# Linear attention and a feed-forward layer on one core: k^T v by heads in column halves, matmuls in the gaps of the head, additions on GpSimd, other urgencies for the planner

## The chip, the cores and the metric

The kernel runs on one core of one Trainium2 chip. The metric is the device time of that core in microseconds, the median of several executions. The engines are TensorE (PE in the profile, its weight loads apart as PEld), VectorE (DVE), ScalarE (ACT), GpSimd (POOL) and SyncE (SP), which issues most transfers.

## The reference

Eight batches of eight heads, 576 positions, head dimension 64. `q`, `k` and `v` are float32, the two weight matrices come in as float64.

```python
q_s = softmax(q, axis=-1)              # over the head dimension
k_s = softmax(k, axis=2)               # over the positions
kv = np.einsum('bhsd,bhse->bhde', k_s, v)          # 64 x 64 for each head
attn = np.einsum('bhsd,bhde->bhse', q_s, kv)
x = attn.transpose(0, 2, 1, 3).reshape(4608, 512)
h = np.maximum(x @ w_in, 0.0)          # w_in 512 x 2048
out = h * h @ w_out                    # w_out 2048 x 512
```

## The kernel before

The output is made in nine tiles `t` of 512 rows: the first 512 positions of each of the eight batches, and a last tile of the eight tails of 64 positions. A tile runs over 16 slices `f` of 128 columns of the hidden layer. For one slice, `first` makes `h` with 12 matmuls, `split_g` squares it and splits it into a high and a low part `gh`, `gl`, and `second` adds 12 matmuls into the four accumulators `acc` of the tile. Each factor is a sum of two float32r parts, and three products of parts are added: that is where the 12 come from. While tile `t` runs, the attention of batch `t + 1` is prepared between its slices (`step`, `step_after`), one pair of heads `p` in four slices.

`kv_product` makes k^T v for such a pair: it multiplies the exponentials of `k` (128 positions by 2 x 64 columns, in `ek`) with `v` of both heads, over four chunks of 128 positions and one more for the tail. The 128 x 128 result holds the two heads' products on its diagonal, and the other two blocks are not used. From batch 1 on, `v` carries a column of ones between its heads (129 columns), so that the sums of the softmax come out of the same matmul. These factors are plain float32; the profile shows each such matmul as two passes.

The weights come as 64-bit words (`load_words`) and are turned into two float32r parts in 16 units: `scale_words` on ACT, `join_words` (a shift and a bit merge on DVE, then an addition of 32-bit integers), `split_words` (a cast on ACT, a subtraction on POOL). In half of the units (even ones), the addition of the first half runs on DVE (`on_vector`), all others on POOL.

Everything up to the end of the loop over slices of tile 0 is recorded and not issued: batch 0's attention ("the head" below), the words, tile 0 and batch 1's attention. `Planner.run` gives every recorded piece a start time from its costs, taking of the pieces that could start next on an engine the one with the longest way to the end (`tail`), and then issues all pieces in the order of these starts. All later code is issued in the order in which it stands. So each engine works through one fixed list, and a piece late in it waits for all before.

The head, for each of four pairs: `first_max` turns `k` with four PE transposes (`kT`), `first_exp` takes exponentials (ACT), `first_turn` turns them back (`ek`, and `ekt` for the tail), `q_norm` and `q_turn` do the same for `q` (`qT`), `kv_product`, and `x_product` (six matmuls of 288 columns) gives a quarter of tile 0's `x`. Line 99 of the profile is the helper that issues every recorded or direct call.

Of the kernel before, what the change touches and what calls it, by code (L numbers as in the profile page):

```python
# [2 lines left out]

# [6 lines left out]
F32 = mybir.dt.float32  # L10
# [103 lines left out]
class Node:  # L114


    def __init__(self, engine):
        self.engine, self.calls, self.busy, self.moved = engine, [], 0.0, 0
        self.before, self.after, self.soon = {}, {}, []
        self.buffers, self.behind = [], None  # L120
        self.start = self.end = self.tail = None


class Planner:
# [3 lines left out]

    HOP = 0.12
    ISSUE, LAND, RATE = 0.6, 2.0, 330.0  # L130
    WAIT = 0.25

    def __init__(self):
        self.open, self.nodes, self.into, self.chain, self.boot = True, [], None, None, []
        self.marks, self.line = {}, {}
        self.due, self.dues = None, []

    @contextmanager
    def together(self, chained=False):
# [16 lines left out]
    def add(self, engine, call, busy, moved, views):  # L156
        if self.into in (None, "next"):
            node = Node(engine)
            self.nodes.append(node)
            if self.into:  # L160
                self.into = node
        else:
            node = self.into
        if moved and self.line is not None:
            node.behind = self.line.get(engine)
            self.line[engine] = node
        if self.due is not None:
            self.dues.append((node, self.due))
        node.calls.append(call)
        node.busy += busy  # L170
        node.moved += moved
        for view, written in views:
            b = view.buffer
            if not b.users and not b.choices:
                told = b.pool.told.setdefault(b.tag, [])
                depth = b.bufs or b.pool.depth
                b.last = told[-1] if told else None
                b.before = told[-depth] if len(told) >= depth else None
                told.append(b)
            if node not in b.users:  # L180
                b.users.append(node)
                node.buffers.append(b)
                if b.pool is not None and b.pool.early:
                    self.boot.append(node)
            for other, w, touched in b.seen:
                if other is not node and (w or written) and (
                    touched is None or view.touched is None or touched & view.touched
                ):
                    node.before[other] = True
            b.seen.append((node, written, view.touched))  # L190
# [43 lines left out]
            ) and all(self.possible(o, b, known, spare) for o in n.before)  # L234
        return known[n]

    def run(self):
        for n in self.nodes:
            for o in n.before:
                o.after[n] = True  # L240
        for n, f in self.dues:
            n.soon = [self.marks[f]] if f in self.marks else []
        for n in self.nodes:
            self.length(n)
        for n in self.nodes:
            for b in n.buffers:
                if len(b.choices) > 1 and n is not b.users[0]:
                    n.tail = max(n.tail, *[u.tail for u in b.users[1:]])
        left = {n: len(n.before) for n in self.nodes}
        ready = [n for n in self.nodes if not left[n]]  # L250
        free, dma, told = {}, 0.0, []
        self.banks = {}
        while ready:
            able = []
            for n in ready:
                t = free.get(n.engine, 0.0)
                if n.behind is not None:
                    if n.behind.start is None:
                        continue
                    t = max(t, n.behind.start + n.behind.busy)  # L260
                for o in n.before:
                    t = max(t, o.end + (0.0 if o.engine is n.engine and not o.moved else self.HOP))
                for b in n.buffers:
                    if b.placed is not None:
                        continue
                    at, _ = self.place(b)
                    if at is None:
                        break
                    t = max(t, at + self.HOP)
                else:  # L270
                    able.append((t, n))
            t0, n0 = min(able, key=lambda x: x[0])
            t, n = max(
                ((t, n) for t, n in able if n.engine is n0.engine and t <= t0 + self.WAIT),
                key=lambda x: x[1].tail,
            )
            n.start, n.end = t, t + n.busy
            free[n.engine] = n.end
            if n.moved:
                dma = max(dma, n.end) + n.moved / self.RATE  # L280
                n.end = dma + self.LAND
            for b in n.buffers:
                if b.placed is None:
                    b.placed = t
                    if b.choices:
                        b.pool, b.tag = self.place(b)[1]
                        self.banks[b.tag] = float("inf")
            for b in n.buffers:
                if b.choices and all(u.end is not None for u in b.users):
                    self.banks[b.tag] = max(u.end for u in b.users)  # L290
            told.append(n)
            ready.remove(n)
            for o in n.after:
                left[o] -= 1
                if not left[o]:
                    ready.append(o)
        assert len(told) == len(self.nodes)
        self.open = False
        for n in sorted(told, key=lambda n: n.start):
            for call in n.calls:  # L300
                call()

# [2 lines left out]
def attention_ffn(  # L305
# [25 lines left out]
    nc = tc.nc  # L331
# [14 lines left out]
    LA = 2  # L346
    LINE = 5
    SOON = 4
    EARLY = 2
    SH = SQ // 2  # L350
    TB = 2
# [85 lines left out]
    def join_words(f):  # L437
        w = cvt.tile([P, 2, M], I32, tag="w", name=f"w_{f}")
        for h in range(2):
            at = slice(h * M, (h + 1) * M)  # L440
            lo, hi = part(f, I32, 0, [h])[:, at], part(f, I32, 1, [h])[:, at]
            ps = bank(f"up_{f}_{h}", f < EARLY).bitcast(I32)
            to = w[:, h, :].only(h)
            V.tensor_scalar(
                out=ps, in0=hi, scalar1=3, scalar2=None, op0=ALU.logical_shift_left
            )
            on_vector = h == 0 and f % 2 == 0
            V.scalar_tensor_tensor(
                out=ps if on_vector else to, in0=hi, scalar=-(2**31), in1=ps,
                op0=ALU.bitwise_and, op1=ALU.bitwise_or,  # L450
            )
            (V if on_vector else G).tensor_tensor(
                out=to, in0=ps if on_vector else to, in1=lo, op=ALU.add, n=580
            )
# [384 lines left out]
    def kv_product(b, p):  # L839
# [2 lines left out]
        tl, th = tail_of(b, p)  # L842
        ps = bank(f"kv_{b}_{p}", b == 0)
        w = 2 * D if b == 0 else W
        with plan.together():
            for c in range(C):
                T.matmul(
                    out=ps[:, 0:w], lhsT=kr[:, c, :], rhs=vr[:, :, c, :] if b == 0 else vr[:, c, :],
                    start=(c == 0), stop=False, n=4 * w,
                )  # L850
            if b == 0:
                T.matmul(
                    out=ps[:, 0:w], lhsT=made.pop(("ekt", p)),
                    rhs=v_heads[tl, 2 * p:2 * p + 2, 0:D].only(p // 2),
                    start=False, stop=True, n=4 * w,
                )
            else:
                T.matmul(
                    out=ps[:, 0:w],
                    lhsT=made["kt", b][:, th, :].rearrange("p h d -> p (h d)").only(  # L860
                        p % 2, p % 2 + 2
                    ),
                    rhs=v_tail[:, p * (W + 1):p * (W + 1) + W],
                    start=False,
                    stop=True,
                    n=4 * w,
                )
        if b == 0:
            ks, at_of = made.pop(("ks", p)), D
        else:  # L870
# [161 lines left out]
        first_turn(p)  # L1032

    for p in range(NP):
        boot_max(p)
        boot_turn(p)
        boot_exp(p)
        q_norm(0, p, G)
        kv_product(0, p)
        q_turn(0, p)  # L1040
        x_product(0, p, x)
    done = {scale_words: 0, join_words: 0, split_words: 0}

    def convert(work, until):
        for u in range(done[work], min(until + 1, NF)):
            work(u)
            done[work] = u + 1

    for u in range(LINE, NF):
        load_words(u)  # L1050
# [72 lines left out]
                prepare(b, p + 1)  # L1123

    prepare(1, 0)
    x_next = None
    for t in range(B + 1):
        b = t + 1
# [27 lines left out]
                step_after(b, f, x_next)  # L1156
            plan.due = None
        if t == 0:
            plan.run()
        if b <= B:  # L1160
            x = split_x(x_next, b)
        if b + 1 < B:
# [43 lines left out]
```

## Time and profile before

| | |
|---|---|
| median of 3 runs | 895.93 us (894.77 to 896.78) |
| the profiled execution | 895.74 us, its span 893.8 us |
| granted TensorE clock, mean | 0.997 |
| PE busy / DVE / ACT / POOL | 871.8 / 483.6 / 358.6 / 187.1 us |

The span reaches from the first to the last instruction; 1.9 us of the profiled execution lie outside it. The busy share is the time in which an engine has an instruction open: matmuls are pipelined, so the durations of neighbouring ones overlap, and the distance between the starts of two rows says what a matmul costs. A granted clock of 1 is 2.4 GHz, one of 0.5 is 1.2 GHz.

### The profile page before, as it was taken

Reading aid. Unit: us, or ns where it says so; the run is one execution under the profiler, and the core shown is the slowest. Engines: PE = TensorE matmul, PEld = TensorE weight load, DVE = VectorE, ACT = ScalarE, POOL = GpSimd, SP = SyncE. Lnnn points to the kernel's source line nnn. Section 1 sums busy time; section 2 is a strip of 40 time slices with the busy share of each in tenths; the row PEclk is TensorE's granted clock in tenths of the full one; section 3 lists DMA queues with packets and bytes.
Section 4 is the critical chain, followed back from the end, with each engine's and each line's share of the span. In section 5 each row is a group of like instructions: output and inputs, shape, how many; then the busy total and the mean of one; then the engine's idle time right before and its main releaser. Section 6 shows DMA issues by size and latency. Waiting matters only on the chain.

```text
span 893.8 us, 11668 instructions
## 1 busy us (share of the span) xinstructions
PE 871.8 (98%) x4054; PEld 725.0 (81%) x4054; DVE 483.6 (54%) x907; ACT 358.6 (40%) x668; POOL 187.1 (21%) x223
## 2 busy tenths in 40 slices
PE   5899999999999999999999999999999999999997
PEld 3777888888888888888888888888888888888886
DVE  7899996544654456544655555446545522233222
ACT  5788854333433243333433343333433422232221
POOL 4477871111011111111111111110111100000000
PEclk9999999999999999999999999999999999999999
DMA  9991022111321123112321122113211020010002
GB/s 282 383 317 49 23 55 84 39 38 27 92 48 38 38 56 86 38 38 50 83 47 28 36 80 49 38 27 76 65 38 38 9 93 1 0 48 1 1 0 48
DMA packets 140874, 57.84 MB, mean 65 GB/s; under 512 B 115600, under 2 KB 134032, under 8 KB 140688
## 3 DMA queue, kind: packets, MB, share of 16 engines
q1 hardware_dynamic: 139104, 55.79, 23.3%
q10 hardware_dynamic: 1712, 1.31, 0.5%
q8 instruction: 32, 0.52, 0.2%
q14 instruction: 26, 0.21, 0.1%
HBM read 46.14 MB, written 10.49 MB: 63 GB/s over the span
## 4 chain that ended last, share of the span: by engine, by line
PE 91%; DVE 5%; issue 1%; ACT 1%; DMA 0%; ACTq 0%; POOL 0%; DVEq 0%; POOLq 0%
PE h L99 42%; PE acc L99 42%; PE kv L99 4%; PE x L99 3%; DVE up L99 1%; DVE w L99 1%; DVE km L99 1%; DMA q<-in_q_dram 0%; DVE h L99 0%; PE qT L99 0%; DVE gl L99 0%; DVE qt L99 0%; DVE mx L99 0%; ACT raw L99 0%; ACTq L99 0%
## 5 line engine op out<-in xcount | busy, mean ns | idle before, releaser
L99 PE MATMUL h<-xh,w 128*128 128x512 f32 x1152 | 380.3, 393 | 1.9 <-DVE gl L99 1.9
L99 PE MATMUL acc<-w,gh 128*128 128x512 f32 x1152 | 355.6, 390 | 0.0
L99 PEld LDWEIGHTS h<-xh,w 128*128 128x128 f32 x1152 | 216.6, 188 | 48.3 <-DVE gl L99 3.3
L99 PEld LDWEIGHTS acc<-w,gh 128*128 128x128 f32 x1152 | 215.1, 188 | 43.9
L99 PE MATMUL h<-xl,w 128*128 128x512 f32 x576 | 225.0, 391 | 0.3 <-DVE xl L99 0.3
L99 PE MATMUL acc<-w,gl 128*128 128x512 f32 x576 | 224.1, 389 | 0.0
L99 DVE SCALAR_TENSOR_TENSOR h<-h,r 128x512 f32<-128x512 f32 x144 | 99.6, 692 | 120.5 <-ACT r L99 120.1
L99 DVE TENSOR_TENSOR gl<-h,gh 128x512 fp32r<-128x512 f32 x144 | 99.2, 689 | 114.2 <-ACT gh L99 111.4
L99 ACT ACTIVATE r<-h 128x512 f32<-128x512 f32 x144 | 85.5, 593 | 171.0 <-PE h L99 170.8
L99 ACT ACTIVATE gh<-r 128x512 fp32r<-128x512 f32 x144 | 90.6, 629 | 124.2 <-PE acc L99 121.9
L99 PEld LDWEIGHTS acc<-w,gl 128*128 128x128 f32 x576 | 108.1, 188 | 22.7
L99 PEld LDWEIGHTS h<-xl,w 128*128 128x128 f32 x576 | 108.4, 188 | 21.5 <-DVE xl L99 0.6
L99 POOL TENSOR_TENSOR k<-k,kmx 128x512 f32<-128x512 f32 x24 | 30.8, 1283 | 170.5 <-issue 134.1
L99 POOL PARTITION_ALL_REDUCE kmx<-km x24 | 17.4, 725 | 197.7 <-DVE km L99 162.5
L99 ACT ACTIVATE q<-q 128x576 f32<-128x576 f32 (+1 forms) x32 | 21.5, 672 | 88.3 <-DVE q L99 82.9
L99 POOL TENSOR_TENSOR ql<-qT,qh 128x576 fp32r<-128x576 f32 x24 | 34.1, 1422 | 104.3 <-issue 54.7
L99 POOL TENSOR_TENSOR w<-w,w 128x512 fp32r<-128x512 f32 x32 | 41.0, 1300 | 16.7 <-ACT w L99 16.7
L99 PEld LDWEIGHTS kv<-v,ek 128*128 128x128 f32 x256 | 34.8, 199 | 3.5 <-DVE ql L99 1.3
L99 DVE SCALAR_TENSOR_TENSOR bsm<-bsm,sw_s 128x18 f32<-128x18 f32 x24 | 4.6, 191 | 60.9 <-DMA sw_s<-bsm 60.9
L99 ACT CAST qh<-qT 128x576 fp32r<-128x576 f32 (+1 forms) x32 | 20.7, 650 | 41.1 <-DVE qT L99 41.1
L99 PE MATMUL kv<-v,ek 128*128 128x129 f32 (+1 forms) x256 | 35.7, 284 | 1.1 <-DVE ql L99 1.1
L99 ACT ACTIVATE raw<-raw 128x1024 f32<-128x1024 f32 (+1 forms) x32 | 35.7, 1144 | 0.1
(103 smaller groups left out, 649.4 us busy)
## 6 DMA issues: line engine op xcount, KB each, us to landing
k<-in_k_dram SPq DMA_DIRECT2D x32, 256.0 KB, 2.7
raw<-in_moe_w_in_dram SPq DMA_DIRECT2D x16, 512.0 KB, 7.8
raw<-in_moe_w_out_dram SPq DMA_DIRECT2D x16, 512.0 KB, 9.2
out_dram<-o SPq DMA_DIRECT2D x32, 256.0 KB, 2.4
v<-in_v_dram SPq DMA_DIRECT2D x56, 128.0 KB, 2.9
q<-in_q_dram SPq DMA_DIRECT2D x96, 72.0 KB, 2.3
sw_m<-bmx SPq DMA_DIRECT2D x96, 2.2 KB, 1.7
sw_s<-bsm SPq DMA_DIRECT2D x96, 2.2 KB, 1.7
```

What stands on the lines that cost most here:

```text
L99: getattr(self.eng, op)(*map(real, args), **{k: real(a) for k, a in kwargs.items()})
```

## The change

`kv_product` makes each chunk with two matmuls instead of one: each takes the 64 columns of one head from `ek` and the 64 (or 65, with the ones) columns of that head from `v`, and writes rows 0 to 63 or 64 to 127 of the result. The two take their places in two column halves of TensorE's array. A product is then 10 matmuls of 64 stationary columns, in place of 5 of 128, and the unused blocks are not made. The planner's cost for them is halved in the same way.

`join_words` does all additions on GpSimd (`on_vector` is always false).

The planner gets three things. Its urgencies (`tail`) are shifted by random amounts on 32 random stretches of its list, given by fixed seeds. Where its plan has TensorE idle ahead of a piece, up to the first matmul of the first `h`, it issues transposes of the identity matrix into a PSUM tile that nothing reads (`fill`), as many as fit the planned gap at 0.25 us each in the first gap and 0.14 us each later. `STEP` and `EASE` are zero, so `ease` does nothing.

```diff
+    READY, COLD, FILL, SPARE = 1.0, 0.25, 0.14, 0.2
...
+    def shift(self, seed):
+        r = random.Random(seed)
+        at, size, by = r.randrange(len(self.nodes)), r.randint(1, 40), r.gauss(0.0, 5.0)
+        for n in self.nodes[at:at + size]:
+            n.tail += by
...
+        first, free = min(m.start for m in self.marks.values()), self.READY
         for n in sorted(told, key=lambda n: n.start):
+            if n.engine is self.marks[0].engine and n.start <= first:
+                fill(int((n.start - free - self.SPARE) / (self.FILL if free > self.READY else self.COLD)))
+                free = n.end
             for call in n.calls:
                 call()
...
+    SEEDS = (1,6,7,10,14,16,17,42,48,79,152,157,158,195,310,373,389,455,905,9005,9006,9011,9012,9022,9044,9049,9071,9080,9087,9120,9132,9219,9227)
...
-            on_vector = h == 0 and f % 2 == 0
+            on_vector = False
...
+            parts = [(kr[:, c, :], vr[:, c, :]) for c in range(C)] + [(ekt, v_tail[:, at:at + W])]
+
+        n = D if b == 0 else D + 1
         with plan.together():
-            for c in range(C):
-                T.matmul(
-                    out=ps[:, 0:w], lhsT=kr[:, c, :], rhs=vr[:, :, c, :] if b == 0 else vr[:, c, :],
-                    start=(c == 0), stop=False, n=4 * w,
-                )
+            for i, (k_part, v_part) in enumerate(parts):
+                for j in range(2):
+                    rows, cols = slice(j * D, (j + 1) * D), slice(j * D, j * D + n)
+                    T.matmul(
+                        out=ps[rows, cols], lhsT=k_part[:, rows],
+                        rhs=vr[:, j, i, :] if b == 0 else v_part[:, cols],
+                        start=(i == 0), stop=(b > 0 and i == C), n=2 * n,
+                    )
...
+    def fill(n):
+
+        for _ in range(n):
+            nc.tensor.transpose(out=idle[:, 0:P], in_=ident, identity=ident)
```

TensorE's list begins with batch 0's transposes; the digit behind `k_` and `qn_` is the pair of heads. Before:

```order
L99 MATMUL kT_131<-ident,k_0_110 128x128 x4
L99 MATMUL ktT<-ident,kt_114 128x128 x2
L99 MATMUL kT_153<-ident,k_1_120 128x128 x4
L99 MATMUL ek_177<-ident,k_0_110 128x128 x4
L99 MATMUL ekt_186<-ident,kt_114 128x128
L99 MATMUL ek_217<-ident,k_1_120 128x128 x4
L99 MATMUL qT_0_238<-ident,qn_0_223 128x128 x4
L99 MATMUL qT_1_249<-ident,qn_1_234 128x128 x4
L99 MATMUL ekt_268<-ident,kt_114 128x128
L99 MATMUL kv_0_285<-v_0_126,ek_0_188 128x128 x4
L99 MATMUL kv_0_285<-v_tail,ekt_279 128x128
```

And with the change, over the same stretch:

```order
L1173 MATMUL idle<-ident 128x128 x9
L100 MATMUL kT_141<-ident,k_0_111 128x128 x4
L1173 MATMUL idle<-ident 128x128 x4
L100 MATMUL ktT<-ident,kt_115 128x128 x2
L1173 MATMUL idle<-ident 128x128 x3
L100 MATMUL kT_170<-ident,k_1_121 128x128 x4
L1173 MATMUL idle<-ident 128x128 x27
L100 MATMUL ek_240<-ident,k_0_111 128x128 x4
L100 MATMUL ekt_250<-ident,kt_115 128x128
L1173 MATMUL idle<-ident 128x128 x11
L100 MATMUL ek_284<-ident,k_1_121 128x128 x4
L100 MATMUL qTt_294<-ident,qt_117 128x128 x2
```

There are 84 such fillings in all, 54 of them ahead of the second `ek`, 30 more in three places behind the first two products. Both products of the first two pairs now stand one behind the other.

In later batches the list keeps its order, and only the product changes. This is pair 2 of batch 2, before:

```order
L99 MATMUL acc_3_1712<-w_1094,gh_8_2033 128x512 x2
L99 MATMUL acc_3_1712<-w_1094,gl_8_2035 128x512
L99 MATMUL kv_2_2120<-v_2_1934,ek_2_2072 128x129 x4
L99 MATMUL kv_2_2120<-v_tail,kt_1489 128x129
L99 MATMUL h_11_2137<-xh_0_1551,w_1094 128x512
```

and with the change:

```order
L100 MATMUL acc_3_1837<-w_1176,gh_8_2168 128x512 x2
L100 MATMUL acc_3_1837<-w_1176,gl_8_2170 128x512
L100 MATMUL kv_2_2255<-v_2_2069,ek_2_2207 64x65 x8
L100 MATMUL kv_2_2255<-v_tail,kt_1627 64x65 x2
L100 MATMUL h_11_2277<-xh_0_1676,w_1250 128x512
```

Five matmuls with 128 stationary columns have become ten with 64; what stands ahead and behind is the same.

On VectorE the first unit of words stood between the sums of `q` in the head (`up` is the shifted word, `w` the merged one, `ISA` the addition on DVE):

```order
L99 TENSOR_REDUCE sm_2_236<-q_2_124 128x8
L99 TENSOR_SCALAR up_1_247<-raw_137 128x512
L99 TENSOR_SCALAR up_0_256<-raw_137 128x512
L99 SCALAR_TENSOR_TENSOR w_262<-raw_137,up_1_247 128x512
L99 SCALAR_TENSOR_TENSOR up_0_256<-raw_137,up_0_256 128x512
L99 ISA w_262<-raw_137,up_0_256 128x1024
L99 COPY ekt_279<-ekt_186 64x128
L99 TENSOR_REDUCE sm_3_283<-q_3_128 128x8
```

and it now stands behind them:

```order
L100 COPY ekt_297<-ekt_250 64x128
L100 COPY ekt_303<-ekt_299 64x128
L100 SCALAR_TENSOR_TENSOR ks_0_205<-ks_0_205 128x1
L100 RECIPROCAL ks_0_205<-ks_0_205 128x1
L100 TENSOR_REDUCE sm_2_317<-q_2_125 128x8
L100 TENSOR_REDUCE sm_3_331<-q_3_129 128x8
L100 TENSOR_SCALAR sm_3_331<-sm_3_331 128x8
L100 RECIPROCAL sm_3_331<-sm_3_331 128x8
L100 TENSOR_SCALAR up_0_356<-raw_147 128x512
L100 SCALAR_TENSOR_TENSOR w_362<-raw_147,up_0_356 128x512
L100 TENSOR_SCALAR up_1_367<-raw_147 128x512
L100 SCALAR_TENSOR_TENSOR w_362<-raw_147,up_1_367 128x512
```

What the first two products need (`ekt`, `ks`) has moved ahead of the words, and the addition has left this engine.

## Rows read from the trace of the kernel before

**Rows 1.** The page's line of busy time: us, share of span, instructions.
```profile
PE 871.8 (98%) x4054; PEld 725.0 (81%) x4054; DVE 483.6 (54%) x907; ACT 358.6 (40%) x668; POOL 187.1 (21%) x223
```

**Rows 2.** Stretches: us, then busy by engine (instructions), clock, DMA share, GB/s.
```profile
10.00:42.00 32.00, 25.40 (x121) 20.27 (x121) 29.01 (x72) 24.71 (x56) 16.47 (x23) 0.95 1.07 368
42.00:138.00 96.00, 92.65 (x441) 75.75 (x442) 88.78 (x158) 71.77 (x108) 73.75 (x70) 1.00 0.39 116
138.00:410.00 272.00, 272.00 (x1281) 228.05 (x1280) 146.59 (x279) 100.37 (x199) 43.82 (x56) 1.00 0.21 49
```

**Rows 3.** TensorE's timeline around one product of batch 3: start, us, instructions.
```profile
321.14 0.39 PE L99 MATMUL acc<-w,gl 128*128 128x512 f32 x1
321.37 1.05 PE L99 MATMUL kv<-v,ek 128*128 128x129 f32 x8
322.26 0.39 PE L99 MATMUL kv<-v_tail,kt 128*128 128x129 f32 x2
322.40 0.48 PE L99 MATMUL h<-xh,w 128*128 128x512 f32 x1
322.71 0.40 PE L99 MATMUL h<-xl,w 128*128 128x512 f32 x1
```

**Rows 4.** Groups by line and form: busy us, mean ns of one, idle before.
```profile
L99 PE MATMUL kv<-v,ek 128*128 128x129 f32 x224 | 29.6, 274 | 0.0
```

**Rows 5.** TensorE's timeline in the head, idle time ahead in brackets.
```profile
9.99 1.11 PE L99 MATMUL ek<-ident,k 128*128 128x128 f32 x4
...
14.40 1.11 PE L99 MATMUL ek<-ident,k 128*128 128x128 f32 x4 [3.08 <-ACT k L99]
15.69 2.13 PE L99 MATMUL qT<-ident,qn 128*128 128x128 f32 x8 [0.18 <-POOL qn L99]
18.09 0.47 PE L99 MATMUL ekt<-ident,kt 128*128 128x128 f32 x1 [0.27 <-ACT ek L99]
18.36 2.00 PE L99 MATMUL kv<-v,ek 128*128 128x128 f32 x8
20.29 0.79 PE L99 MATMUL kv<-v_tail,ekt 64*128 64x128 f32 x2
21.01 0.69 PE L99 MATMUL qTt<-ident,qt 128*128 128x128 f32 x2
21.49 1.91 PE L99 MATMUL kv<-v,ek 128*128 128x128 f32 x8
...
24.06 1.05 PE L99 MATMUL kT<-ident,k 128*128 128x128 f32 x4
24.82 0.42 PE L99 MATMUL x<-qh,kvh 128*128 128x288 f32 x1
25.08 0.30 PE L99 MATMUL x<-ql,kvh 128*128 128x288 f32 x1
25.21 0.29 PE L99 MATMUL x<-qh,kvl 128*128 128x288 f32 x1
...
29.93 1.16 PE L99 MATMUL kv<-v,ek 128*128 128x128 f32 x8 [1.09 <-DVE ql L99]
31.02 0.48 PE L99 MATMUL kv<-v_tail,ekt 64*128 64x128 f32 x2
31.43 0.86 PE L99 MATMUL kT<-ident,k 128*128 128x128 f32 x4
```

**Rows 6.** Stretches of 2 us (columns as in group 2).
```profile
30.00:32.00 2.00, 2.00 (x15) 1.76 (x15) 1.89 (x7) 1.39 (x3) 0.00 (x0) 0.94 1.05 395
32.00:34.00 2.00, 2.00 (x11) 1.98 (x10) 1.95 (x5) 0.70 (x3) 1.43 (x2) 0.50 1.06 406
34.00:36.00 2.00, 2.00 (x12) 1.75 (x11) 1.34 (x3) 1.45 (x5) 0.28 (x2) 0.71 1.09 404
```

**Rows 7.** Groups by line and form: the additions of the words.
```profile
L99 POOL TENSOR_TENSOR w<-w,raw 128x512 int32<-128x512 int32 x24 | 31.3, 1312 | 8.4 <-DVE w L99 4.1 <-ACT ek L99 1.7 <-ACT qh L99 1.5
L99 DVE CUSTOM_DVE_ANT_0 w<-raw,up 128x1024 uint16<-128x1024 uint16 x8 | 5.4, 681 | 0.3
```

More of the change, by code (lines that the diff above doesn't have):

```diff
@@ L1 @@
 import itertools
+import random
 from contextlib import ExitStack, contextmanager
@@ L121, in __init__ @@
         self.start = self.end = self.tail = None
+        self.since = 0.0
 class Planner:
@@ L136, in __init__ @@
         self.due, self.dues = None, []
+        self.ease = 0.0
     @contextmanager
@@ L166, in add @@
             self.line[engine] = node
+        node.ease = self.ease
         if self.due is not None:
@@ L235, in possible, with prepare @@
         return known[n]
-    def run(self):
+    def prepare(self):
         for n in self.nodes:
@@ L248, in run, with order @@
                     n.tail = max(n.tail, *[u.tail for u in b.users[1:]])
+        for n in self.nodes:
+            n.tail -= n.ease
+    def order(self):
         left = {n: len(n.before) for n in self.nodes}
+        for n in self.nodes:
+            n.since, n.start, n.end = 0.0, None, None
+            for b in n.buffers:
+                b.placed = None
         ready = [n for n in self.nodes if not left[n]]
@@ L255, in run @@
             for n in ready:
-                t = free.get(n.engine, 0.0)
+                t = max(free.get(n.engine, 0.0), n.since)
                 if n.behind is not None:
@@ L260, in run @@
                     t = max(t, n.behind.start + n.behind.busy)
-                for o in n.before:
-                    t = max(t, o.end + (0.0 if o.engine is n.engine and not o.moved else self.HOP))
                 for b in n.buffers:
@@ L294, in run @@
                 left[o] -= 1
+                o.since = max(
+                    o.since, n.end + (0.0 if o.engine is n.engine and not n.moved else self.HOP)
+                )
                 if not left[o]:
                     ready.append(o)
+        return told
+    def shift(self, seed):
[3 more added lines that the diff above has]
+            n.tail += by
+    def run(self, seeds, fill):
+        self.prepare()
+        for seed in seeds:
+            self.shift(seed)
+        told = self.order()
         assert len(told) == len(self.nodes)
         self.open = False
+        first, free = min(m.start for m in self.marks.values()), self.READY
         for n in sorted(told, key=lambda n: n.start):
+            if n.engine is self.marks[0].engine and n.start <= first:
+                fill(int((n.start - free - self.SPARE) / (self.FILL if free > self.READY else self.COLD)))
+                free = n.end
             for call in n.calls:
@@ L348, in attention_ffn @@
     SOON = 4
+    STEP = 0.0
+    SEEDS = (1,6,7,10,14,16,17,42,48,79,152,157,158,195,310,373,389,455,905,9005,9006,9011,9012,9022,9044,9049,9071,9080,9087,9120,9132,9219,9227)
+    EASE = 0.0
     EARLY = 2
@@ L844, in kv_product @@
         w = 2 * D if b == 0 else W
-        with plan.together():
-            for c in range(C):
-                T.matmul(
-                    out=ps[:, 0:w], lhsT=kr[:, c, :], rhs=vr[:, :, c, :] if b == 0 else vr[:, c, :],
-                    start=(c == 0), stop=False, n=4 * w,
-                )
-            if b == 0:
[L852 to L867, printed above, removed]
+        if b == 0:
+            ekt = made.pop(("ekt", p))
+            parts = [(kr[:, c, :], None) for c in range(C)]
+        else:
+            ekt = made["kt", b][:, th, :].rearrange("p h d -> p (h d)").only(p % 2, p % 2 + 2)
+            at = p * (W + 1)
+            parts = [(kr[:, c, :], vr[:, c, :]) for c in range(C)] + [(ekt, v_tail[:, at:at + W])]
+        n = D if b == 0 else D + 1
+        with plan.together():
+            for i, (k_part, v_part) in enumerate(parts):
[5 more added lines that the diff above has]
+                        start=(i == 0), stop=(b > 0 and i == C), n=2 * n,
+                    )
+            if b == 0:
+                for j in range(2):
+                    rows = slice(j * D, (j + 1) * D)
+                    T.matmul(
+                        out=ps[rows, rows], lhsT=ekt[:, rows],
+                        rhs=v_heads[tl, 2 * p + j, 0:D].only(p // 2),
+                        start=False, stop=True, n=2 * n,
+                    )
         if b == 0:
@@ L1034, in attention_ffn @@
     for p in range(NP):
+        plan.ease = p * STEP
         boot_max(p)
@@ L1041, in attention_ffn @@
         x_product(0, p, x)
+    plan.ease = 0.0
     done = {scale_words: 0, join_words: 0, split_words: 0}
@@ L1045, in convert @@
         for u in range(done[work], min(until + 1, NF)):
+            plan.ease = EASE if 0 < u < 4 else 0.0
             work(u)
             done[work] = u + 1
+        plan.ease = 0.0
     for u in range(LINE, NF):
@@ L1125, in attention_ffn @@
     prepare(1, 0)
+    idle = ps_h.pool.tile([P, M], F32, tag="h", name="idle")
+    def fill(n):
+        for _ in range(n):
+            nc.tensor.transpose(out=idle[:, 0:P], in_=ident, identity=ident)
     x_next = None
@@ L1158, in attention_ffn @@
         if t == 0:
-            plan.run()
+            plan.run(SEEDS, fill)
         if b <= B:
```

## The prediction

> **What bounds the kernel.** I read the page's line of busy time first: TensorE is busy for 871.8 of 893.8 us, and no other engine for more than 54% [rows 1]. Then I cut the span at the places where the work changes [rows 2]. From 138 to 410 us TensorE is busy in all of 272.00 us while VectorE needs 146.59: in the tiles behind the first, time leaves the kernel only as time on TensorE. From 42 to 138 us, in which tile 0 runs and the words are still converted, TensorE lacks 3.35 us and VectorE is busy for 92% (88.78 of 96). From 10 to 42 us, in the head, TensorE has something open in 25.40 of 32 us and VectorE in 29.01, which leaves VectorE 3.0 us.
>
> The clock has to be read from the matmuls. The granted clock is shown as 1 at first, but eight passes of a product take 2.00 us from 18.36, and eight of the same shape 1.16 from 29.93; the six matmuls for `x` follow each other by 0.26 us up to 25.08 and by 0.13 from there [rows 5]. So TensorE ran at the lower of its two levels, 1.2 GHz, until about 25 us, and the column of the clock knows nothing of that stretch. It fell to 0.50 once more around 33 us, behind a stretch with gaps, and came back in the two microseconds after 34 [rows 6].
>
> **The products from batch 1 on.** There are 28, each of 4 chunks and a tail; the 224 passes of the chunks [rows 4] are 28 x 4 x 2. In rows 3 eight passes start at 321.37 and the next at 322.26: 0.111 us each. From the first pass to the `h` behind it go 1.03 us, and that `h` takes 0.31 to the next start where its neighbours in a row take 0.23 (321.14 to 321.37): 0.08 more. A product costs 1.03 + 0.08 = 1.11 us.
>
> The change makes 20 passes of 65 columns from 10 of 129. By columns one takes 0.111 x 65/129 = 0.056 us. No row shows two matmuls in the array at the same time, so the cost is bounded from both sides: all 20 one behind the other take 1.12 us, and in pairs, each half of the array on its own, 10 x 0.056 = 0.56.
>
> The place in the array has a price too. In the head, the tail's passes use 64 of the 128 rows. There the row of eight ends at 31.09 and the tail starts at 31.02, 0.07 ahead; in batch 3 it starts 0.16 ahead of the end (322.42 against 322.26). So going into the part of the array costs 0.09. The way back: `kT` starts 0.07 ahead of the tail's end (31.43 against 31.50), and in batch 3 the next row 0.25 ahead (322.40 against 322.65), of which the different kind of matmul may be a part: up to 0.18, and I take 0.09 again [rows 3, 5]. This is for halves of the rows; for halves of the columns I take the same. With the first load of weights no longer hidden behind a matmul, half a pass or 0.05, and the 0.08 of the first `h` still there, a paired product costs 0.56 + 0.18 + 0.05 + 0.08 = 0.87 and saves 0.24. Times 28: **-6.7 us**. Without the price of the place it would save 1.11 - 0.64 = 0.47, or 13.2 us; one pass after the other it would cost 1.12 + 0.31 = 1.43 and lose 0.32, or 9.0 us. I take the paired value: the moving columns of a pair need no more than the rate that float32r matmuls already reach (288 columns in 0.13 us against 129 in 0.111, rows 3 and 5). The unused blocks were never read, so leaving them out costs nothing.
>
> The Trainium skill (TensorEngine Tiling, section Tiling Modes, Key Properties) says that tiles operate independently, weight loads and matmuls in parallel, and that a change of mode drains TensorE. The 0.09 us above agrees with the second; no row here shows the first, and if it holds with a free drain, the 13.2 us are the gain.
>
> **The head.** From 18.09 to 24.82 TensorE goes without a gap through two products, seven transposes at half speed. At full speed a product takes 1.50 (29.93 to 31.43) and a transpose 0.11, together 3.8 of these 6.7 us: 2.9 to gain. The second slow stretch, some 3.3 us, would give 1.6, so 4.5 in all [rows 5, 6]; the halves could add 4 x 0.24 = 1.0. VectorE caps this: it has 3.0 us of idle time in the whole head. Its list moves `ekt` and `ks` ahead of the first words and gives one addition away, so it no longer stands in the way at 18 to 20 us, but the words moved back must still be made. I take **-3.0**, between 0 and -5.5.
>
> The 84 fillings come on top. Cold, a transpose takes 0.24 (2.13 us for eight, less the overlap), warm 0.11. The nine ahead of the first transpose and the seven behind it fit the gaps that were there. The 27 stand where `ek` came 0 us behind its forerunner, at 9.99; warm they take 3.0 and `ek` starts at about 13, still ahead of 14.40, when the second `ek` was ready. The 11 fall into that gap of 3.08 [rows 5]. So they cost nothing while the clock is up, the cover being VectorE's and ACT's work, which those transposes wait for.
>
> **The additions.** Eight on VectorE take 5.4 us (681 ns), on GpSimd 1312 ns each, 10.5 us [rows 7]. Seven of them lie behind 42 us: VectorE falls from 88.78 to 84.0, GpSimd rises from 73.75 to 82.9 of 96 [rows 2]. What TensorE can gain there is its 3.35 us of idle time; I take **-1.5**, between 0 and -3.35, since a longer addition (0.63 us) delays each unit's cast and subtraction. The list of SP moves batch 1's first loads past a few words; transfers run at 368 GB/s up to 42 us and at 116 behind it, and words are used until 138, so I cost that at nothing; were it not covered, the 0.45 MB of these loads would take 1.2 us at that rate.
>
> **Sum.** 895.7 (the profiled execution, 0.2 below the median of the three runs) - 6.7 - 3.0 - 1.5 = **884.5 us**.
>
> **The rivals.** *The halves take turns* (slower): if weights or matmuls of the second half wait for the first, a product costs 1.43 and the kernel 895.7 + 9.0 - 4.5 = 900.2. It decides as soon as a pass costs more than 0.048 us: then 28 x (20 x 0.048 + 0.31 - 1.11) eats the 4.5 of the other parts. For it speaks that weight loads are open for 725.0 us [rows 1] and that twenty loads of 64 columns bring as many columns as ten of 128: if loads set the pace, halves save nothing. Against it, that those 725.0 us lie beside matmuls here.
>
> *The fillings do not wake the clock.* From 9.99 to 18.3 the rows show 17 transposes, from 14.40 nearly without a gap, and the products behind them still ran at 1.2 GHz [rows 5]. Then 38 fillings ahead of the second `ek` take 9.1 us, of which a gap of 3.08 was there: up to 6.0 late, and nothing gained from the clock. VectorE has words to do meanwhile, so I take half, +3.0: 895.7 - 6.7 + 3.0 - 1.5 = 890.5. The Trainium skill (TensorE: Matmul & The Clock Gate, Part 4: PE-mode transpose) says just that: transposes do not count as busy in the same way, and the full clock does not come on. The trace bears it out only so far, since those transposes had gaps. By that rule the time would be the 890.5.
>
> *The plan is worse than the old one.* The shifts are random numbers; GpSimd at 86% makes subtractions late, and TensorE waits for low parts. The head and tile 0 lose 4 in place of winning 4.5: 893.5, near no change.
>
> **How the numbers follow.** Chances: forecast 0.50, no waking 0.25, turns 0.18, worse plan 0.07. The forecast alone spans 877 (13.2 us for the products, 5.5 for the head, nothing for the additions) to 889. The range has to take in no waking and the worse plan, and the lower edge of the turns, which I put at 898: **877 to 898**. A difference of 0.2%, 1.8 us, is about what a measurement can tell from none. Faster: 0.50 + 0.22 of no waking + 0.03 of a worse plan = 0.75; same 0.06; slower 0.19.
>
> **What would show it.** Right: ten rows of passes with 64 columns in some 0.6 us, the `h` behind them within 0.8 us of the first pass; the head's products at full speed from the first one, and all of tile 0 some 3 us earlier; VectorE below 85 us in its 96. Wrong: passes 0.056 apart (turns), fillings 0.24 apart up to the products (no waking), or waits of `h` and `acc` for `w` on GpSimd (worse plan). The forecast fails above all if a pass of half the columns has a floor that this trace, whose shortest pass is 128 columns, does not show.

## The result, and the profile after

The changed kernel takes 886.31 us (median of 4 runs, 885.49 to 886.73) against 895.94 for the kernel before in the same comparison: a ratio of 0.9892, 95% interval 0.9875 to 0.9909. The profiled execution took 886.37 us, its span 884.6 against 893.8.

The page's line of busy time and the three stretches of [rows 1, 2], after:

```profile
PE 869.6 (98%) x4458; PEld 714.1 (81%) x4458; DVE 477.1 (54%) x899; ACT 357.7 (40%) x668; POOL 197.8 (22%) x231
```

```profile
10.00:42.00 32.00, 28.28 (x240) 22.74 (x239) 31.21 (x77) 27.30 (x61) 21.80 (x27) 1.00 1.09 375
42.00:138.00 96.00, 94.08 (x498) 76.50 (x497) 85.66 (x155) 73.14 (x112) 79.30 (x76) 1.00 0.38 116
138.00:410.00 272.00, 272.00 (x1416) 223.76 (x1415) 147.38 (x283) 100.94 (x200) 46.77 (x60) 1.00 0.22 51
```

From 10 to 42 us VectorE is now busy for 31.21 of 32 us; from 42 to 138 TensorE lacks 1.92 us in place of 3.35. The only waits of TensorE from 42 to 140 us (engine, line and what it waited for; us in total, times, longest) are:

```profile
PE kmT L100 <- DVE km L100: 1.6, 1, 1.6
PE h L100 <- DVE gl L100: 0.3, 1, 0.3
```

TensorE's timeline around a product of batch 3, which answers to [rows 3]:

```profile
313.63 0.39 PE L100 MATMUL acc<-w,gl 128*128 128x512 f32 x1
313.95 0.69 PE L100 MATMUL kv<-v,ek 128*64 128x65 f32 x16
314.46 0.29 PE L100 MATMUL kv<-v_tail,kt 128*64 128x65 f32 x4
314.68 0.50 PE L100 MATMUL h<-xh,w 128*128 128x512 f32 x1
315.02 0.39 PE L100 MATMUL h<-xl,w 128*128 128x512 f32 x1
```

Sixteen passes of 65 columns now start within 0.51 us: two of them every 0.058 us (single starts of a pair lie 6 to 7 ns apart), where one pass of 129 took 0.111.

To see where the 9.2 us of span went, I cut every trace at three starts: the first `acc`, the last `acc` of tile 0, the last `acc` of all. Lengths in us, with the results of all runs:

| kernel | first `acc` at | tile 0 | after it | median (range) | ratio to before (95%) |
|---|---|---|---|---|---|
| before | 47.98 | 95.96 | 744.58 | 895.94 | 1 |
| after | 45.72 | 92.07 | 740.80 | 886.31 (885.49 to 886.73) | 0.9892 (0.9875 to 0.9909) |
| e1_halves_only | 46.82 | 95.58 | 739.83 | 889.67 (889.43 to 891.31) | 0.9932 (0.9917 to 0.9946) |
| e2_no_fill | 45.70 | 92.09 | 740.22 | 885.82 (885.55 to 886.63) | 0.9884 (0.987 to 0.9897) |
| e3_halves_in_turn | 45.80 | 94.23 | 749.41 | 897.21 (896.46 to 897.74) | 1.001 (1.0001 to 1.0019) |
| e4_whole_products | 46.43 | 93.61 | 745.02 | 891.81 (891.38 to 892.57) | 0.995 (0.9937 to 0.9962) |
| e5_no_shifts | 47.94 | 93.59 | 740.31 | 888.66 (888.39 to 888.88) | 0.991 (0.9897 to 0.9924) |
| e6_adds_on_vector | 46.50 | 97.07 | 740.40 | 891.89 (891.32 to 893.36) | 0.9949 (0.9936 to 0.9962) |
| e7_fill_only | 49.63 | 95.99 | 744.34 | 895.04 (894.86 to 897.08) | 0.9985 (0.9976 to 0.9994) |
| e8_first_fills | 45.63 | 92.14 | 739.95 | 885.35 (884.98 to 885.88) | 0.9882 (0.987 to 0.9895) |
| e9_adds_only | 46.24 | 94.05 | 744.36 | 891.23 (891.0 to 891.88) | 0.994 (0.9928 to 0.9953) |
| e10_shifts_only | 48.36 | 95.62 | 744.83 | 895.51 (893.49 to 897.73) | 0.9993 (0.9982 to 1.0004) |
| e11_adds_old_order | 47.26 | 98.55 | 745.92 | 899.51 (898.0 to 901.15) | 1.004 (1.0028 to 1.0052) |
| e12_halves_and_adds | 50.34 | 93.61 | 740.29 | 890.92 (889.53 to 891.26) | 0.9942 (0.993 to 0.9954) |

After against before: 2.26 us up to the first `acc`, 3.89 in tile 0 and 3.78 behind it, less 0.75 by which the stretch behind the last `acc`, with the final write to memory, is longer: 9.2. (That stretch takes 5.7 to 6.2 us in the five kernels with after's order, which are after, e2, e3, e4 and e8, and 5.2 to 5.6 in the others; why stays open.) Behind tile 0, six tiles still prepare a batch. Measured from the last `acc` of the tile ahead to its own, such a tile takes 95.04 us with whole products and 94.27 with halves in pairs. In most executions single tiles take longer, in after one of them by 1.1 us. The profiled execution of e7 is its longest of eleven, 2 us over its median, so its first column isn't used. Each ratio is against runs of before on the same chip, with medians of 895.89 (e1 to e4), 896.85 (e5, e6, e7, e9) and 896.13 (e8, e10 to e12); single runs of before lay between 894.5 and 898.13.

### The profile page after: what moved, and what is told of

It is laid out like the page before. It is cut to its first block, busy times and chain, and to the rows that moved or that the text cites. A ratio compares the mean times of both kernels' runs of the same rounds, so it can differ in the third digit from the quotient of the medians.

```text
span 884.6 us, 12464 instructions
## 1 busy us (share of the span) xinstructions
PE 869.6 (98%) x4458; PEld 714.1 (81%) x4458; DVE 477.1 (54%) x899; ACT 357.7 (40%) x668; POOL 197.8 (22%) x231
## 3 DMA queue, kind: packets, MB, share of 16 engines
q10 hardware_dynamic: 1712, 1.31, 0.5%
## 4 chain that ended last, share of the span: by engine, by line
PE 91%; DVE 4%; DMA 1%; SPq 1%; issue 1%; ACT 0%; DVEq 0%; ACTq 0%
PE h L100 43%; PE acc L100 43%; PE x L100 2%; PE kv L100 2%; SPq L100 1%; DVE w L100 1%; DVE up L100 1%; DMA raw<-in_moe_w_in_dram 1%; DMA k<-in_k_dram 0%; DVE gl L100 0%; DMA sw_m<-bmx 0%; DVE kc L100 0%; DVE h L100 0%; DVE sm L100 0%; DVE km L100 0%
## 5 line engine op out<-in xcount | busy, mean ns | idle before, releaser
L100 POOL TENSOR_TENSOR w<-w,raw 128x512 int32<-128x512 int32 x32 | 41.6, 1315 | 6.2 <-ACT raw L100 2.8
L100 ACT ACTIVATE kvh<-kv,ks 64x64 fp32r<-64x64 f32 x64 | 19.7, 308 | 29.0 <-DVE ks L100 27.7
```

Of the source, the lines that this page charges most:

```text
L100: getattr(self.eng, op)(*map(real, args), **{k: real(a) for k, a in kwargs.items()})
```

## The experiments

Apart from its edit, each kernel is the one that it starts from. None leaves out work that the output needs.

**The products: e1 and e4.** e1 is the kernel before with the products in halves; the planner's cost is written so that it gets the same number for a product as before, and so makes the same order. e4 is the kernel after with whole products, again with an unchanged cost (and so the order of after).

```diff
# e1, on before
+                        out=ps[rows, cols], lhsT=k_part[:, rows],
+                        rhs=vr[:, j, i, :] if b == 0 else v_part[:, cols],
+                        start=(i == 0), stop=(b > 0 and i == C), n=2 * w - 15.6,
# e4, on after
+                    out=ps[:, 0:w], lhsT=kr[:, c, :], rhs=vr[:, :, c, :] if b == 0 else vr[:, c, :],
+                    start=(c == 0), stop=False, n=4 * (D if b == 0 else D + 1) + 31.2,
```

> The kernel before with the products in halves and nothing else: every engine keeps its order. If the halves run in pairs, as the trace of the changed kernel reads (passes start two at a time, pairs 0.058 us apart), each of the 28 later products costs 0.93 in place of 1.12 us: 5.3 us less, and in the head, where two products still run at 1.2 GHz, 0 to 3 us more on top: 888 to 891 us. If the gain of the change came from the planner's new order, this kernel stays at 894 to 896 us.

> The changed kernel with whole products again, planned at the same cost, so that all orders stay as they are. If the halves give 0.19 us for each of 28 products and up to 0.4 for each of four in the head, the time is 886.3 + 5.3 + 0 to 1.6: 891.6 to 893.2 us, and order, fillings and additions alone are worth 3 to 4 us against the kernel before. If the parts feed each other (halves shorten the head's chain much more), it is 894 us or more.

The halves alone give 6.2 us (889.67 against 895.89), and taking them out of the changed kernel costs 5.5. Both came as expected. Behind tile 0, where TensorE waits for almost nothing (0.5 us in after, nothing listed in before), e1 gains 4.75 us and e4 loses 4.2: 0.18 to 0.20 for each of 24 products, and the 0.77 us between 95.04 and 94.27 are 0.19 for each of a tile's four. The mechanism holds, its size is below the forecast 0.24.

**The halves made to take turns: e3.** The same matmuls, all of the first head ahead of all of the second.

```diff
-            for i, (k_part, v_part) in enumerate(parts):
-                for j in range(2):
+            for j in range(2):
+                for i, (k_part, v_part) in enumerate(parts):
```

> The changed kernel with the ten matmuls of a product sorted by halves: first five for one head, then five for the other. If the gain needs two passes in the array at the same time, a product becomes 20 passes of 0.058 one behind the other, 0.58 us more for each of 28 and the four of the head: about 902 to 905 us. If TensorE takes matmuls of the second half ahead by itself, or if a pass is cheap for another reason, it stays at 886 to 888 us.

It takes 897.21 us, 10.9 more than after and below the 902 to 905 expected. TensorE's timeline of e3 at the same kind of place:

```profile
318.60 0.39 PE L100 MATMUL acc<-w,gl 128*128 128x512 f32 x1
318.92 0.73 PE L100 MATMUL kv<-v,ek 128*64 128x65 f32 x10
319.43 0.22 PE L100 MATMUL kv<-v_tail,kt 128*64 128x65 f32 x1
319.49 0.22 PE L100 MATMUL kv<-v,ek 128*64 128x65 f32 x1
319.49 0.22 PE L100 MATMUL kv<-v_tail,kt 128*64 128x65 f32 x1
319.55 0.46 PE L100 MATMUL kv<-v,ek 128*64 128x65 f32 x5
319.84 0.28 PE L100 MATMUL kv<-v_tail,kt 128*64 128x65 f32 x2
320.05 0.50 PE L100 MATMUL h<-xh,w 128*128 128x512 f32 x1
```

From the first pass to the `h` go 1.13 us in place of 0.73, and 28 x 0.40 = 11.2 agrees with the 10.9. So pairing is what the halves live on: without it their whole gain is lost, and more. The 20 passes were expected to need 20 slots of 0.058; they took 17. The rows show why. The first head has eight passes over the chunks, yet ten such passes stand ahead of its tail at 319.43: the second head's first passes, which the kernel issues later, started beside the first head's last ones. The Trainium skill (TensorE: Matmul & The Clock Gate, Part 3, The mechanism) has matmuls start in strict program order; these rows differ from it, as far as the recorded starts go.

**The fillings: e2, e8 and e7.** e2 is after without all 84 fillings, e8 without the 30 behind the second `ek`, both with the order of everything else unchanged. e7 is before with fillings in the gaps of its own plan.

```diff
# e2
-        for _ in range(n):
+        for _ in range(0):
# e8
+        filled.append(n)
-        for _ in range(n):
+        for _ in range(n if sum(filled) <= 54 else 0):
# e7: after with whole products, their cost as before, and
+    SEEDS = ()
+            on_vector = h == 0 and f % 2 == 0
```

> The changed kernel without the 84 fillings, all else in the same order. If the fillings raise the clock early and the head profits, the clock comes up only after the first products (beyond 18 us, in place of about 10.7) and the time rises by 1 to 4 us: 887.3 to 890.5 us. If VectorE sets the pace of the head, as its 31.2 busy us of 32 say, the fillings buy nothing: 885.5 to 887 us.

> The changed kernel with only the 54 fillings ahead of the second turning of k; the 30 later ones, of which ten lie on the chain of waits for 1.09 us ahead of the first x, are left out. If those ten hold up the head, 885 to 885.8 us. If VectorE hides them, as it hid the lack of all 84, 885.6 to 886.6 us, no difference to 886.3 and 885.8.

> The kernel before with fillings alone, in its own planned gaps; the order of all else is unchanged. Two theories of the head: the forecast's, that the products from 18 to 25 us run at half speed on the way to the end, gives 892.5 to 895 us once the clock comes up near 11 us; that VectorE sets the pace whatever the clock does, as leaving the fillings out of the changed kernel showed (885.8 against 886.3), gives 895 to 897 us. If transposes do not raise the clock at all, it rises no earlier than before (24.9 us), and the time is 896 to 899 us.

The fillings do raise the clock. In the profiled executions the seven kernels with fillings first reach 2.4 GHz at 8.1 to 13.8 us, the seven without at 18.1 to 37.5. TensorE's timeline of after in the head, against [rows 5]:

```profile
1.56 2.18 PE L1173 MATMUL idle<-ident 128*128 128x128 f32 x9 [1.56 <-POOL ident masks.py:199]
...
9.65 3.70 PE L1173 MATMUL idle<-ident 128*128 128x128 f32 x27
13.19 0.60 PE L100 MATMUL ek<-ident,k 128*128 128x128 f32 x4
13.62 0.27 PE L100 MATMUL ekt<-ident,kt 128*128 128x128 f32 x1
13.73 1.36 PE L1173 MATMUL idle<-ident 128*128 128x128 f32 x11
15.50 0.66 PE L100 MATMUL ek<-ident,k 128*128 128x128 f32 x4 [0.40 <-ACT k L100]
...
17.66 0.69 PE L100 MATMUL kv<-v,ek 128*64 128x64 f32 x16
18.28 0.33 PE L100 MATMUL kv<-v_tail,ekt 64*64 64x64 f32 x4
```

The four `ek` transposes take 0.60 us where they took 1.11. Within the 27 fillings, two stretches of 1 us each (busy time and number of fillings) show the step; the column behind, the granted clock, reads 1.00 in both and misses it:

```profile
9.70:10.70 1.00, 1.00 (x5) 1.00 (x5) 1.00 1.22 223
10.80:11.80 1.00, 1.00 (x11) 1.00 (x10) 1.00 1.07 331
```

Five in one microsecond, then eleven: 1.2 GHz up to about 10.7 us, 2.4 GHz behind it, and until then TensorE had run transposes alone, from 9.65 on without a gap. By the Trainium skill (TensorE: Matmul & The Clock Gate, Part 4: PE-mode transpose) they should not have done that; this trace differs.

Yet e2, which has no fillings, takes 885.82 us, no more than after. Its clock comes up without them, at about 18.1 us in the middle of the first product. Two rows of four transposes show it:

```profile
16.64 1.12 PE L100 MATMUL qT<-ident,qn 128*128 128x128 f32 x4
19.61 0.66 PE L100 MATMUL qT<-ident,qn 128*128 128x128 f32 x4
```

So in e2 the first two products, which the forecast wanted at full speed, nearly have it too. Later TensorE does run slowly again for a while (stretches of 2 us; PE, PEld, DVE, ACT, POOL, granted clock, DMA share, GB/s):

```profile
24.00:26.00 2.00, 1.94 (x10) 1.43 (x9) 1.57 (x7) 1.97 (x5) 1.21 (x5) 0.73 1.06 404
26.00:28.00 2.00, 1.72 (x8) 1.73 (x9) 1.92 (x6) 1.42 (x7) 1.72 (x2) 0.50 1.06 401
28.00:30.00 2.00, 2.00 (x15) 1.76 (x14) 1.98 (x4) 1.83 (x7) 1.20 (x3) 0.92 1.06 389
```

But its first `acc` starts at 45.70, that of after at 45.72. In e8 the clock is at 0.50 for longer, from 21.8 to 28.6 us, and its first `acc` starts at 45.63. (Its 885.35 us lie in the range expected if the ten fillings on the chain held the head up, but those 0.09 us are no evidence of that.) The chain of waits says why. This is after's, then e2's, behind the slow stretch:

```profile
36.55 0.70 DVE up L100
...
38.33 0.60 DVE w L100
...
43.41 1.18 DVE w L100 x2
44.59 0.62 DVE h L100
...
59.04 0.64 DVE km L100
...
59.73 0.33 PE kmT L100
```

```profile
36.49 0.69 DVE up L100
...
38.27 0.61 DVE w L100
...
43.34 1.18 DVE w L100 x2
44.53 0.62 DVE h L100
```

In before the chain ran over TensorE here:

```profile
18.56 2.52 PE kv L99 x10
21.08 0.62 PE qTt L99 x2
21.70 2.43 PE kv L99 x10
```

With the change it stays on VectorE from 34 us until `kmT` at 59.73, and behind the slow stretch VectorE does the same things at the same times in both kernels, within 0.07 us. In this order the slow passes of e2 and e8 are not on the way: they fall into time in which TensorE waits for others anyway (in e2 it is busy for 23.78 of the 32 us from 10 to 42). What a clock that stays low through the first two products would cost in this order, no run shows.

Where the plan is another, the clock is on the way: without the shifts, the fillings are worth 2.3 us (e12 890.92, e5 888.66; first `acc` at 50.34 and 47.94). In e12 the clock comes up only at about 37.5 us, in e5 at 12.7, and the chain of e12 runs over these products. From the third to the fourth go 7.70 us in e12 (first two lines) and 5.72 in e5:

```profile
30.95 1.12 PE L100 MATMUL kv<-v,ek 128*64 128x64 f32 x16 [0.36 <-DVE ql L100]
38.65 0.69 PE L100 MATMUL kv<-v,ek 128*64 128x64 f32 x16
30.53 0.69 PE L100 MATMUL kv<-v,ek 128*64 128x64 f32 x16 [0.29 <-DVE ql L100]
36.25 0.69 PE L100 MATMUL kv<-v,ek 128*64 128x64 f32 x16
```

In before's own plan the fillings bring 0.15% (0.9985, 0.9976 to 0.9994), some 1.3 us, at the border between the first two theories of e7. Its products do run at full speed. Why that brings no more, its profiled execution can't say: it is the longest, its clock falls again from 28.0 to 34.8 us, and ScalarE, which the first `x` waits for, is held up by a late transfer of words (in before it starts on the same words at 22.00):

```profile
19.47 1.06 PE L100 MATMUL kv<-v,ek 128*128 128x128 f32 x8
24.46 1.12 ACT L100 ACTIVATE raw<-raw 128x1024 f32<-128x1024 f32 x1 [2.58 <-DMA raw<-in_moe_w_out_dram]
```

**The additions: e9, e11 and e6.** e9 is before with all additions on GpSimd, planned anew. e11 has them on GpSimd too, but the planner is told that they run on VectorE as before, so every engine's order is the old one. e6 is after with the additions back on VectorE, planned anew under the same shifts.

```diff
# e9 on before; e6 on after is the reverse
-            on_vector = h == 0 and f % 2 == 0
+            on_vector = False
# e11, on before: VG issues on GpSimd and is planned as V
+    VG = Engine(plan, nc.gpsimd, 0.11, 0.00113)
+    VG.stand = V
-            (V if on_vector else G).tensor_tensor(
+            (VG if on_vector else G).tensor_tensor(
```

> The kernel before with all additions on GpSimd and nothing else but the new plan that this makes. If VectorE's 5.4 us are on the way in tile 0, 893 to 895 us. If the words only wait longer for GpSimd, 895.5 to 898 us.

> The kernel before with the eight additions issued on GpSimd, but planned as if they still ran on VectorE, so that every engine keeps its old order but for the additions themselves. The additions with a new plan took 4.7 us off (891.2 against 895.9). If that is VectorE's time itself, 891 to 892.5 us here too. If it is the new order that the plan found, this stays at 894.5 to 896.5 us, and part of it, 893 to 894, means both.

> The changed kernel with eight additions back on VectorE, planned anew with the same shifts. If VectorE is what the head and tile 0 wait for, its 5.4 us more lead to 887.5 to 890 us. If the relief of VectorE is given back by GpSimd's longer additions, it stays at 885.5 to 887 us.

e9 gains some 5 us (0.994, 0.9928 to 0.9953), more than either expectation; 1.9 of it lie in tile 0. e11 loses 3.4 (1.004, 1.0028 to 1.0052), more than any of its expectations, although it takes the same additions from VectorE. Where it goes is in the waits of ACT from 10 to 140 us, in e11 and in before:

```profile
ACT w L101 <- POOL w L101: 16.1, 11, 2.8
```

```profile
ACT w L99 <- DVE w L99: 3.4, 3, 1.9
```

In the old order the cast of a unit stands on ACT's list where VectorE's addition of 0.68 us would have been done; GpSimd's takes 1.31 and stands behind other units, and tile 0 becomes 2.6 us longer. So in the old order the late casts cost more than VectorE's 5.4 us bring; what those are worth by themselves, no run separates. The move pays with the order that the planner makes when it knows where the additions run. e6 costs 5.6 us against after, more than the 887.5 to 890 expected, but that is no price of the additions alone: its shifts hit another list.

**The shifts: e5, e10 and e12.** e5 is after without shifts, e12 without shifts and fillings (so the halves and the additions), e10 is before with the shifts alone.

```diff
# e5; e12 has e2's edit too; e10 has e6's edit, whole products and no fillings
-    SEEDS = (1,6,7,10,14,16,17,42,48,79,152,157,158,195,310,373,389,455,905,9005,9006,9011,9012,9022,9044,9049,9071,9080,9087,9120,9132,9219,9227)
+    SEEDS = ()
```

> The changed kernel with the 32 random shifts left out of the planner's urgencies; halves, additions and fillings (as many as this plan's gaps take) stay. If the head and tile 0 owe their 4 us to the shifted order, the time rises to 888.5 to 890.5 us, near that of the halves alone (889.7). If they owe them to the additions on GpSimd, it stays at 886 to 887.5 us.

> The kernel before with the 32 shifts alone: whole products, eight additions on VectorE, no fillings. If the shifts are worth their 2.3 us (886.3 against 888.7 without them) in any plan, 893 to 894.5 us. If they only suit the plan they were drawn for, 895 us or more, also above the kernel before.

> Halves and additions alone, without shifts and fillings. With fillings this plan took 888.7 us. If fillings are worth nothing here either, 888.3 to 889.2 us; if they helped only where the order was not tuned, 890 us or more.

The list holds 33 seeds, so 33 shifts and not 32. Shifts alone change nothing that the runs can tell (0.9993, 0.9982 to 1.0004). In after they are worth 2.3 us with the fillings and 5.1 without (e12 to e2), all of it in the first two columns of the table. They seem to belong to the one list that they were drawn for. The parts don't add up either: the halves alone give 6.2 us and the additions alone some 5, both together 5.2 (e12), where the first `acc` starts only at 50.34, with the clock low until about 37.5 us.

## Why the prediction came out as it did

The forecast was 884.5 us; 886.31 lies in its range, 1.8 above it. That it is so near is partly luck: the products came out 1.4 us and the head 0.7 below their terms, the final stretch took 0.75 that no term has, and tile 0 gave 1.6 more than the term for the additions.

- **The products, forecast -6.7: right in its mechanism, 0.05 us a product too large.** Worked out again from the rows of after: going into the halves costs 0.09 (313.63 to 313.95 is 0.32, before it was 0.23 in [rows 3]), as forecast. From the first pass to `h` go 0.73 (313.95 to 314.68): by the single starts in the trace 0.58 for ten pairs (0.56), 0.05 for the first weights (0.05) and 0.10 for the way back (0.09). The first `h` costs 0.11 more than its neighbours (0.08). Together 0.93 against 0.87, and the old product measured so costs 1.12: 0.19 saved, 28 x 0.19 = 5.3 us. No single term failed; three are one to three hundredths too small. One support was a little generous: 130 columns in 0.056 us are 2.3 a nanosecond, the `x` rows that the prediction compares with have 2.2 (288 in 0.13), and the pairs came out at 2.2. The independent tiles of the Trainium skill (TensorEngine Tiling, Key Properties) are in these rows. A free change of mode, with which the gain would have been 13.2, is not.
- **The head, forecast -3.0: near in size (first `acc` 2.26 us earlier), its reason not borne out in the new order.** The step was that the clock, up early, gives 4.5 us of which VectorE allows 3.0. The clock does come up, at about 10.8 us, but e2 reaches the first `acc` at the same time with a clock that rises at 18.1 and falls again from 24.9 to 28.3. What failed is the step from TensorE's slow passes in [rows 5] to the end: in before they were on the chain, and there an early clock is worth some 1.3 us (e7); in the new order VectorE's list is, and passes that are slow from 21.8 to 28.6 us cost nothing (e8). That the fillings cost nothing was right (e8 and e2 differ from after by less than 1 us), and `ek` behind the 27 starts at 13.19, forecast about 13.
- **The additions, forecast -1.5: too small, and half right in its reason.** TensorE's idle time from 42 to 138 us, which the forecast counted, fell by 1.43, from 3.35 to 1.92. But tile 0 is 3.89 us shorter, of which four products give 0.8; that leaves 3.1, inside the stated 0 to 3.35. VectorE fell to 85.66, not to 84.0, because other work of its list now lies behind 42 us, and GpSimd rose to 79.30, not 82.9, because six additions in place of four now lie ahead of it. The gain came only with the new order (e9 against e11).
- **The halves take turns**: refuted by pairs every 0.058 us in the trace, and e3 shows what it would have been, 897.21 (forecast 900.2; fewer slots were needed).
- **The fillings do not wake the clock**: refuted by the eleven fillings in the microsecond behind 10.8, and by the earlier rise in all seven kernels that have them.
- **The plan is worse than the old one**: not this plan (and its sum, 895.7 - 6.7 + 4, is 893.0, not 893.5), but it was the rival to take more seriously. e11 comes near it, with long waits for `w` on GpSimd, though of ScalarE's casts and not of `h` and `acc`, and e12 has a late head.

What stays open: how much of the 2.26 us of the head belongs to each edit, since the additions and the shifts each make another plan by themselves (halves alone 1.16, additions alone 1.74, shifts alone a loss of 0.4), and of tile 0's 3.89 us the 1.7 that neither TensorE's idle time (1.4 less) nor four products (0.8) explain. No version is clearly better than after: e8 (885.35) and e2 (885.82) lie within what separates runs of it.

## What to carry to other kernels

Two matmuls that use half of TensorE's columns each run at the same time when they are issued in turn, half by half; with float32 factors and 65 columns a pair of passes then costs 0.058 us where one whole pass costs 0.111. That is 0.53 us over a product of ten, but entering and leaving the halves took back 0.34 of it. Grouping such matmuls should save part of that; no run here tried it. Before you speed up an engine, see which engine the chain runs over in the new order, not in the old: fillings that brought the clock up at 12.7 us in place of 37.5 were worth 2.3 us in one order, and at 10.8 in place of 18.1 nothing in another. Where a planner makes the order, an operation that is moved to another engine has to be known to it: the same move was worth some 5 us with a new plan and cost 3.4 with the old.

## What was unexpected of the hardware

Transposes alone brought TensorE from 1.2 to 2.4 GHz (a row of 27, 5 of them in one microsecond and then 11). Matmuls of one column half started ahead of earlier-issued ones of the other half (e3, ten passes ahead of the tail at 319.43). And the first matmul of the whole array behind the halves took 0.34 us to the next start, 0.11 more than its neighbours, although the way back had been paid ahead of it; behind a whole product in before it was 0.08 more.
